# Two layers of attention and FFN on one core: query blocks of 256, value matmuls taken late in a pass through a shared bank, a shorter rsqrt

## Chip, core and metric

One core of a Trainium2 chip. The metric is the device time of one execution in microseconds (us). Ratios are the mean time of one kernel's fast runs over that of the other's fast runs of the same rounds, so not quite the ratio of the medians quoted beside them. A difference under 2%: "same"; intervals are 95%.

Spans come with a mean granted TensorE clock (1.0 is full speed). In profiles PE is TensorE's matmuls, PEld its weight loads, DVE is VectorE, ACT ScalarE and POOL GpSimd.

## The reference

Two layers, each an attention half and an FFN half, on x of 2048 rows by 448, bfloat16, with the same weights in both layers.

```python
x = x + A(layernorm(x))     # 16 heads of 28: softmax(q k^T / sqrt(28)) v, then @ wo
x = x + B(layernorm(x))     # relu(x @ w1 + b1)^2 @ w2 + b2, inner width 1792
```

Each layer has 16 x 2048 x 2048 scores to exponentiate: over two layers 134 million, in tiles of 128 rows 1.05 million columns, which is 683 instructions of 128x1536 (the last of 128x1024).

## The kernel before

A planner inside the kernel places every instruction in order of estimated time. The streams have priorities: scores 0, exponentials 1, value matmuls 2, and the rest ("chains" of projection, layernorm and FFN of a block) from 3 on; junk matmuls, which only keep TensorE's clock up, come last. Four heads make a group g; a "pass" is one block of queries and one g over a range of keys. W1 and W2 stand for the two products of the FFN, rsqrt for the reciprocal square root in the layernorm, and a bank is a unit of PSUM, the memory that the matmuls here write to; the pools below hold eight. The code is abridged:

```python
blocks = [[(0, 4), (4, 4), (8, 4), (12, 4)],            # first tile, tiles of 128 queries
          [(0, 4), (4, 4), (8, 2), (10, 2), (12, 1), (13, 1), (14, 1), (15, 1)]]
ps_sc = tile_pool(bufs=2, PSUM)   # scores, 3 banks each
ps_o  = tile_pool(bufs=1, PSUM)   # one bank for value matmuls
ps_m  = tile_pool(bufs=1, PSUM)   # one bank for QKV, projection, FFN, junk
...
def engs_now(early=False):        # who empties a bank of QKV / W1
    return ("ACT", "DVE") if (early and ("s", 0) not in pl.tok) or len(s_left) == 0 else ("DVE",)
...
def rsqrt(e):                     # 12 instructions on 128 x (1 to 4)
    nc.vector.tensor_scalar(out=v, in0=mv[:, 0:nt, 1], scalar1=EPS, op0=ALU.add)
    nc.vector.tensor_scalar(out=yi, in0=v.bitcast(DT.int32), scalar1=1, op0=ALU.arith_shift_right)
    nc.vector.tensor_scalar(out=yi, in0=yi, scalar1=-1.0, scalar2=float(MAGIC), op0=ALU.mult, op1=ALU.add)
    for _ in range(3):
        nc.vector.scalar_tensor_tensor(out=t, in0=y, scalar=-0.5, in1=y, op0=ALU.mult, op1=ALU.mult)
        nc.vector.tensor_tensor(out=t, in0=t, in1=v, op=ALU.mult)
        nc.vector.scalar_tensor_tensor(out=y, in0=t, scalar=1.5, in1=y, op0=ALU.add, op1=ALU.mult)
...
def e_stream():                   # one exponential over three score banks
    nc.scalar.activation(out=pt[:, 0:n], in_=gbuf[gi]["sc"][:, 0:n], func=AF.Exp, scale=scale)
...
def p_stream():                   # value matmuls of a step as soon as its exponential is done
    o = Op("PE", 0.23 + 0.01 * r, fn, deps=[("e", gis[-1]), ...], acq=R_o if opens else None, ...)
...
def heat():                       # junk matmuls where the planned load falls short
    for gi in range(1, len(groups)):
        short = 0.74 - pl.load(WINDOW)          # WINDOW = 2.8 us
        if short <= 0 or not s_left: continue
        k = 1 if short < 0.14 else 2            # matmuls of 448 columns
```

The softmax here doesn't subtract the row's maximum and nothing guards it: scores larger than these inputs give would overflow.

## Time and profile before

| | median us | spread | profiled span us | clock |
|---|---|---|---|---|
| before | 965.8 | 965.59 to 966.02 | 962.6 | 0.993 |

The prediction below reads the page of this profile: the exponentials on ScalarE run without a break for most of the span. I cut the span at the seventh exponential (27.73 us), after which they run on, and at the end E of the last one (938.98 us). Busy time by these three stages, kernel before; the columns are the stretch, its length, then busy us and instructions of PE, PEld, DVE, ACT and POOL, the TensorE clock, the DMA share and GB/s:

```profile
0.00:27.73 27.73, 23.30 (x131) 10.28 (x134) 20.23 (x71) 14.28 (x14) 7.53 (x16) 1.00 0.82 241
27.73:938.98 911.25, 812.99 (x7962) 304.42 (x8011) 402.58 (x915) 909.60 (x678) 0.00 (x0) 1.00 0.04 11
938.98:962.60 23.62, 17.96 (x174) 12.96 (x173) 10.62 (x32) 5.31 (x11) 0.00 (x0) 0.84 0.05 16
```

The clock column reads 1.00 in the head only because the trace's clock records begin at about 6.2 us: from 1.2 to 6.0 us the first matmuls come every 0.37 us, afterwards every 0.19.

The middle stage is full: 909.60 of 911.25 us on ScalarE. Only the 27.73 and the 23.62 us at the ends and the 1.65 us of gaps can be saved by anything that leaves the exponentials as they are.

### The profile page before, as it was taken

The numbers are of one execution on the slowest core, as the hardware profiler recorded it, in microseconds if no ns is written. First come the engines' busy times: TensorE is split into PE (matmuls) and PEld (weight loads), VectorE is DVE, ScalarE is ACT, GpSimd is POOL, SyncE is SP. The second block draws the span as 40 slices with busy tenths as digits, with TensorE's granted clock in tenths as the row PEclk, the third lists the DMA queues.
The fourth block names the chain that finished last, engine by engine and source line by source line (L and its number), as shares of the span: only waits on it lengthen the run. The fifth ranks groups of instructions, "written<-read, shape, count | busy, mean of one in ns | idle before, by whom it ended". The sixth has DMA issues, their size and how long they took to land.

```text
span 962.6 us, 19338 instructions
## 1 busy us (share of the span) xinstructions
PE 854.3 (89%) x8267; PEld 327.7 (34%) x8318; DVE 433.4 (45%) x1016; ACT 929.2 (97%) x701; POOL 7.5 (1%) x16
## 2 busy tenths in 40 slices
PE   8888899899888998888888999898899889988987
PEld 3333223233232332322323233223233333555555
DVE  7843335434354344653445433325525433444454
ACT  5999999999999999999999999999999999999992
POOL 3000000000000000000000000000000000000000
PEclk9999999999999999999999999999999999999998
DMA  9000010000000000000000000010000000000000
GB/s 276 2 1 1 2 41 7 12 12 13 13 12 1 12 13 13 1 1 1 1 1 1 1 1 1 12 36 24 12 22 17 13 18 22 17 21 13 22 10 16
DMA packets 24642, 17.25 MB, mean 18 GB/s; under 512 B 11754, under 2 KB 21547, under 8 KB 24556
## 3 DMA queue, kind: packets, MB, share of 16 engines
q1 hardware_dynamic: 24556, 16.02, 5.6%
q8 instruction: 65, 1.06, 0.5%
q14 instruction: 21, 0.17, 0.1%
HBM read 13.73 MB, written 2.06 MB: 16 GB/s over the span
## 4 chain that ended last, share of the span: by engine, by line
ACT 68%; issue 18%; PE 12%; DVE 1%; ACTq 0%
ACT pt L558 68%; PE mt L417 4%; PE sc L543 3%; PE oT L593 2%; PE sc L417 1%; PE oT L233 1%; PE mt L763 1%; DVE r L719 1%; PE tp L359 0%; DVE xnT L369 0%; DVE rec L641 0%; DVE x_sb L690 0%; PE den L635 0%; ACT r L717 0%; ACT Q_sb L431 0%
## 5 line engine op out<-in xcount | busy, mean ns | idle before, releaser
L558 ACT ACTIVATE pt<-sc 128x1536 bf16<-128x1536 f32 (+1 forms) x683 | 917.8, 1729 | 6.6 <-PE sc L543 6.5
L543 PE MATMUL sc<-Q_sb,K_sb 32*128 32x512 bf16 (+2 forms) x3072 | 269.2, 309 | 53.8 <-ACT pt L558 45.1
L593 PE MATMUL oT<-pt,V_sb 128*32 128x512 bf16 (+2 forms) x3072 | 206.1, 316 | 1.0 <-ACT pt L558 0.6
L543 PEld LDWEIGHTS <-K_sb 32*128 32x128 bf16 x3072 | 98.3, 91 | 298.9 <-issue 287.3
L417 PE MATMUL mt<-xnT,w 128*128 128x512 bf16 (+2 forms) x565 | 116.6, 321 | 16.7 <-DVE r L719 10.7
L719 DVE TENSOR_SCALAR r<-mt 128x512 bf16<-128x512 f32 x106 | 72.8, 686 | 127.2 <-PE mt L417 127.1
L417 PE MATMUL mt<-w,h 128*128 128x448 bf16 x434 | 102.9, 355 | 2.5 <-DVE x_sb L690 1.0
L593 PEld LDWEIGHTS <-V_sb 128*32 128x32 bf16 x3072 | 62.6, 94 | 110.2 <-issue 103.9
L690 DVE TENSOR_TENSOR x_sb<-x_sb,mt 128x448 bf16<-128x448 bf16 x62 | 38.5, 620 | 136.5 <-PE mt L417 136.0
L763 PE MATMUL mt<-xn,ident 128*128 128x448 bf16 x204 | 68.0, 356 | 9.9 <-DVE xnT L369 1.5
L417 PEld LDWEIGHTS <-w 128*128 128x128 bf16 x672 | 51.3, 101 | 57.0 <-issue 42.1
L417 PEld LDWEIGHTS <-h 128*128 128x128 bf16 x448 | 35.2, 97 | 45.4 <-issue 23.9
L726 DVE TENSOR_TENSOR h<-r 128x512 bf16<-128x512 bf16 x114 | 47.5, 418 | 5.6 <-ACT r L717 2.5
L417 PE MATMUL mt<-xnT,wq 128*128 128x512 bf16 x115 | 34.5, 380 | 7.2 <-DVE Q_sb L433 4.1
L310 DVE BATCH_NORM_STATS2 st<-x_sb 128x6 f32<-128x448 bf16 x64 | 39.7, 621 | 2.2 <-DMA x_sb<-in_A_x_dram 0.8
L433 DVE CAST Q_sb<-mt 128x512 bf16<-128x512 f32 x30 | 20.7, 689 | 37.5 <-PE mt L417 37.4
L433 DVE CAST K_sb<-mt 128x512 bf16<-128x512 f32 x29 | 20.0, 691 | 36.1 <-PE mt L417 36.1
L459 DVE CAST V_sb<-mt 128x448 bf16<-128x448 f32 x31 | 19.3, 621 | 33.7 <-PE mt L417 33.7
L417 PE MATMUL mt<-xnT,wk 128*128 128x512 bf16 x103 | 30.2, 381 | 3.4 <-DVE K_sb L433 0.9
L369 DVE COPY xnT<-tp 128x1024 bf16<-128x1024 bf16 (+1 forms) x31 | 20.8, 672 | 27.2 <-PE tp L359 27.2
L417 PE MATMUL mt<-wo,oTn 128*128 128x448 bf16 x124 | 30.0, 354 | 2.5 <-DVE x_sb L690 1.2
L417 PE MATMUL mt<-wv,xnT 128*128 128x448 bf16 x124 | 29.9, 360 | 2.6 <-DVE V_sb L459 2.0
(75 smaller groups left out, 330.7 us busy)
## 6 DMA issues: line engine op xcount, KB each, us to landing
rec<-scr SPq DMA_DIRECT2D x20, 256.0 KB
x_sb<-in_A_x_dram SPq DMA_DIRECT2D x8, 224.0 KB
out_dram<-x_sb SPq DMA_DIRECT2D x16, 112.0 KB
w<-in_B_w_dram SPq DMA_DIRECT2D x1, 1568.0 KB
w<-in_B_w_dram SPq DMA_DIRECT2D x1, 1344.0 KB
rec<-scr SPq DMA_DIRECT2D x8, 128.0 KB
rec<-scr SPq DMA_DIRECT2D x12, 64.0 KB
part_sb<-in_A_wqkv_dram SPq DMA_DIRECT2D x1, 672.0 KB
```

Of the source, the lines that this page charges most:

```text
L310: nc.vector.bn_stats(out=st[:, :], in_=x_sb[:, t0 + j, :])
L369: nc.vector.tensor_copy(out=dst, in_=tp[:, :, 0:w])
L417: nc.tensor.matmul(box["t"][:, c0:c0 + n], lhsT=lhsT, rhs=rhs, start=a, stop=b)
L433: nc.vector.tensor_copy(out=dst, in_=src)
L459: nc.vector.tensor_copy(out=o, in_=i)
L543: nc.tensor.matmul(sc[:, c0:c0 + nt * P], lhsT=K_sb[l][rows, g, (kb + i) * P:(kb + i + 1) * P], rhs=Q_sb[rows, g, t0 * P:(t0 + nt) * P], s ...
L558: nc.scalar.activation(out=pt[:, 0:n], in_=gbuf[gi]["sc"][:, 0:n], func=AF.Exp, scale=scale)
L593: nc.tensor.matmul(box["t"][DHP * hh:DHP * hh + DHP, 0:n], lhsT=V_sb[l][:, kb + i, 4 * g + hh, :], rhs=gbuf[gi]["pt"][:, c0:c0 + n], start ...
L690: nc.vector.tensor_tensor(out=x_sb[:, tb, :], in0=x_sb[:, tb, :], in1=t[:, 0:D], op=ALU.add)
L719: nc.vector.tensor_scalar(out=r[:, 0:w], in0=t[:, 0:w], scalar1=0.0, scalar2=None, op0=ALU.max)
L726: nc.vector.tensor_tensor(out=h[:, 0:w], in0=r[:, 0:w], in1=r[:, 0:w], op=ALU.mult)
L763: nc.tensor.matmul(t[:, 0:D], lhsT=ident[:, :], rhs=xns[0][:, 0:D], start=True, stop=True)
```

## The change

Its intent, as I read it: shorter blocks give finer work to place, a bank bound to value matmuls becomes a second bank for everything, and VectorE's layernorm gets shorter. It also brings code for a polynomial exponential on VectorE, which is switched off (LAST = 0 lets no group take it). It also changes constants of the planner (SLACK from 0.6 to 0.4, GATE, AHEAD) and several buffer counts. The diff, cut to its core and in places shortened:

```diff
+QR = 256
-MAGIC = 0x5F3759DF
+MAGIC = 0x5F1FFFF9
+LAST = 0            # no exponential on VectorE
+NPT = 11            # buffers of exponentials (before: 4)
+AEND = 8            # ScalarE helps to empty banks until score group 8
+HOLD = 3            # value matmuls wait for 3/8 of a pass ...
+CHUNK = 2           # ... and come two steps at a time
-    blocks = [[(0, 4), (4, 4), (8, 4), (12, 4)], [(0, 4), (4, 4), (8, 2), (10, 2), (12, 1), ... (15, 1)]]
+    blocks = [[(0, 2), (2, 2), ... (14, 2)], [(0, 2), (2, 2), ... (10, 2), (12, 1), (13, 1), (14, 1), (15, 1)]]
-    ps_o = ctx.enter_context(tc.tile_pool(name="ps_o", bufs=1, space=bass.MemoryType.PSUM))
-    ps_m = ctx.enter_context(tc.tile_pool(name="ps_m", bufs=1, space=bass.MemoryType.PSUM))
+    ps_m = [ctx.enter_context(tc.tile_pool(name=f"ps_m{i}", bufs=1, ...)) for i in range(2)]
     def engs_now(early=False):
-        return ("ACT", "DVE") if (early and ("s", 0) not in pl.tok) or len(s_left) == 0 else ("DVE",)
+        return ("ACT", "DVE") if (early and ("s", AEND) not in pl.tok) or len(s_left) == 0 else ("DVE",)
     # rsqrt: 12 instructions become 8
-            nc.vector.tensor_scalar(out=v, in0=mv[:, 0:nt, 1], scalar1=EPS, ...)
-            nc.vector.tensor_scalar(out=yi, ..., op0=ALU.arith_shift_right)
-            nc.vector.tensor_scalar(out=yi, in0=yi, scalar1=-1.0, scalar2=float(MAGIC), ...)
-            for _ in range(3):
+            nc.vector.tensor_scalar(out=v, ..., scalar1=EPS, scalar2=-0.5, op0=ALU.add, op1=ALU.mult)
+            nc.vector.tensor_scalar(out=y.bitcast(DT.int32), in0=v.bitcast(DT.int32), scalar1=-0.5,
+                                    scalar2=float(MAGIC - 2 ** 22 - 2 ** 30), op0=ALU.mult, op1=ALU.add)
+            for k, c in ((1.407904506, 1.6819139), (None, 1.5)):      # three instructions each
...
     def first_block(blk):
-        ... layernorm(4 * blk, 4, ...)
+        ... layernorm(2 * blk, 2, ...)
     # exponentials: log2(e) * 2**23 is folded into Q when its bank is emptied
-                nc.scalar.activation(..., func=AF.Exp, scale=scale)
+                nc.scalar.activation(..., func=AF.Exp, scale=float(np.log(2.0)) * 2.0 ** -23)
     # values
+            hold = 0 if end else max(gi for gi, _, _ in todo[min(HOLD * len(todo) // 8, len(todo) - 1)][1])
+            yield Op("-", 0.0, None, deps=[("e", hold)])
+            while todo:
+                now = [t for t in todo if there(t[1])][:some]         # some = CHUNK
...
-                   acq=R_o if opens else None,
+                       acq=None if "o" in box else pools_now(),
```

## The prediction

> **What bounds the kernel now.** I read the page's busy shares first, then ScalarE alone in order of time, then the chain that ended last, then TensorE around the places where ScalarE stood still.
>
> ```profile
> PE 854.3 (89%) x8267; PEld 327.7 (34%) x8318; DVE 433.4 (45%) x1016; ACT 929.2 (97%) x701; POOL 7.5 (1%) x16
> ACT 68%; issue 18%; PE 12%; DVE 1%; ACTq 0%
> L558 ACT ACTIVATE pt<-sc 128x1536 bf16<-128x1536 f32 (+1 forms) x683 | 917.8, 1729 | 6.6 <-PE sc L543 6.5
> ```
>
> ScalarE is busy 97%, and 917.8 of its 929.2 us is one line: 683 exponentials over three score banks at once. They overlap (683 x 1729 ns is more than 917.8 us), so the pitch, not the mean, is what one costs. The third line also says that in the whole run the exponentials waited only 6.6 us. ScalarE in order of time shows where:
>
> ```profile
> 15.07 6.82 ACT L558 ACTIVATE pt<-sc 128x1536 bf16<-128x1536 f32 x5 [0.49 <-PE sc L543]
> 26.39 463.80 ACT L558 ACTIVATE pt<-sc 128x1536 bf16<-128x1536 f32 x345 [4.49 <-PE sc L543]
> 490.97 428.80 ACT L558 ACTIVATE pt<-sc 128x1536 bf16<-128x1536 f32 x319 [0.78 <-PE sc L543]
> 920.50 18.48 ACT L558 ACTIVATE pt<-sc 128x1536 bf16<-128x1536 f32 x14 [0.73 <-PE sc L543]
> ```
>
> The pitch is 463.80/345 = 1.3443 us. So the span of 962.6 us has three parts: a head until the stream runs without a break (26.39 us, with five exponentials done in it), the stream (678 exponentials, to 938.98), and a tail of 962.6 - 938.98 = 23.6 us with no exponential. The time of 965.8 us is 3.2 us over the span.
>
> The two breaks of 0.7 us deserve a look, TensorE at the first:
>
> ```profile
> 486.54 0.40 PE L593 MATMUL oT<-pt,V_sb 128*32 128x512 bf16 x4
> 487.56 0.61 PE L543 MATMUL sc<-Q_sb,K_sb 32*128 32x512 bf16 x3 [0.62 <-ACT pt L558]
> 488.65 1.67 PE L417 MATMUL mt<-wv,xnT 128*128 128x448 bf16 x4
> 491.04 0.92 PE L417 MATMUL mt<-wv,xnT 128*128 128x448 bf16 x4 [0.17 <-DVE V_sb L459]
> ```
>
> The same four matmuls take 1.67 us and two microseconds later 0.92: TensorE ran at half pace after a stretch in which it did only 0.39 + 0.40 us of work per 1.34 us. The second break (920 us) has the same picture. The junk matmuls of line 763 (204, 68.0 us) are there to prevent this.
>
> [...]
>
> **The change, part by part.**
>
> *Exponentials.* The diff adds a polynomial exponential on VectorE, but its guard asks for a group at or beyond 60 and at most 0, so no group takes it. The order of instructions confirms it: ScalarE still has 682 exponentials of 1536 columns and one of 1024. Folding log2(e) into Q moves a factor. Gain in the stream: 0. That leaves a floor of 682 x 1.344 + 0.95 = 917.7 us, and puts the only possible gains into the 21 us of head, 1.5 us of breaks and 23.6 us of tail.
>
> *Blocks of 256.* Score and value matmuls go from 1536 of 512 columns + 512 of 256 + 1024 of 128 each (3072) to 3584 of 256 + 1024 of 128 (4608): more instructions, same columns. The kernel before already runs this size at 690 to 910 us: six score matmuls of 256 columns take 0.39 us, as three of 512 do, and ScalarE is 100% busy there. So no cost by itself.
>
> *Head.* Only two tiles are normalised first and the rsqrt has 8 instructions, not 12, at about 0.2 us each. I follow it with the durations of before. Statistics of three tiles 3.50 to 5.8; rsqrt 0.2 + 0.35 + 6 x 0.195 = 1.7, to 7.5; the fourth tile's statistics 0.8; two norms 0.7, to 8.95. In the old trace the fourth step would be the transposes at once, but the 34 warm-up matmuls hold TensorE until 10.1 in both kernels, and VectorE's queue has the second block's rsqrt (1.7) ahead of the copy. Copy 10.65 to 11.35, against 12.03 before. From there to the first exponential it was 3.0 us; so 14.4 against 15.07. Then ScalarE does five more copies among the exponentials (K, two V, Q; 0.6 each), and scores queue behind QKV matmuls; by the same durations the sixth exponential starts at about 24.2 and the seventh at 27.3, after which I see no more waits for K or Q. Before, the sixth started at 26.39, so the seventh at 27.73. Gain 0.4 us; the early start is mostly eaten.
>
> *Stream.* From 27.3: 676 x 1.3443 + 0.95 = 909.7, end at 937.0 without breaks. The value matmuls are now withheld until 3/8 of a pass and issued two steps at a time (16 matmuls, 2 x 0.33 us), and the filler goes from 204 to 345. I summed TensorE's work between neighbouring score groups in both orders, with pitches from the trace (0.33 us a value step, 0.19 for 448 columns, 0.11 for 256, 0.36 for a score group): the mean is 1.18 us before and 1.20 after, of 1.344, but carrying over what does not fit, the backlog exceeds 0.5 us at 24 groups before and 83 after, and 0.9 us [...] at 0 and 3. Bunching makes it lumpier. The second shared bank lets FFN matmuls go on while VectorE empties the first, which spares waits of 11 us in all (behind line 719) that did not delay ScalarE. I put the breaks at 2 us, against 1.5. End of stream 939.0.
>
> *Tail.* Before, from the end of the stream E: four rounds of denominators through one bank, the projection of the last block added at E + 6.2, 12 rsqrt instructions with two squares of the block before among them (norm done at E + 11), and W1 only at E + 14.1 because TensorE had W2 of block 14 first. After, block 14's W1 is nearly all done inside the stream. From E: 8 left-over W1 matmuls 0.6, one filler 0.35, two value steps 0.85 (before 0.4 for one), copy 0.3, denominator and reciprocal 1.5, multiply 0.3, meanwhile W2 of block 14 (3.0), projection 0.9, addition done at E + 7.1: later by 0.9. Statistics 0.85, rsqrt 8 x 0.19 = 1.55, norm 0.4, transposes 0.45, copy 0.6: W1 at E + 11.05, earlier by 3.05. Then W1 3.1, W2 3.0, addition 0.6, store 2.7: 20.7. But TensorE now idles from E + 6.5 to E + 10 before W1, while before W2 of block 14 kept it warm. [...] Tail 22.3, against 23.6.
>
> Sum: 939.0 + 22.3 = 961.3 span, + 3.2 = 964.5 us. Against before that is -0.4 in the head, +0.5 in breaks and -1.3 in the tail: -1.2 (with rounding -1.3).
>
> **The rivals.** (a) *TensorE lags in the stream.* For it: backlog at 83 groups, and each spell at half pace cost 0.75 us before. Against: more filler, spare mean, two banks. Five to fifteen such breaks would make 968 to 976; being over 985 would take some 27. (b) *Better overlap in head and tail.* If the tail stays warm and the head has no gap at all, 2 + 3 us more: 959. Nothing lies below: floor 917.7 + at least 12 of head and 16 of tail + 3.2 is 949. (c) *Two banks pay in the stream.* It looks like the intent, but a wait of TensorE that ScalarE did not feel pays nothing; then 964 as said.
>
> **Range and chances.** Head uncertain by 1 us, tail by 2, breaks by -1.5 to +8, skewed upward: 959 to 972. Two per cent is 19.3 us, below 946.5 (under the floor of b) or above 985.1. Faster 0.02, same 0.94, slower 0.04.
>
> **What would show it.** ScalarE in order of time: 683 exponentials with a pitch of 1.344; first at about 14.4; a gap before the seventh that puts it near 27.3; few breaks, each of under 1 us, with TensorE at half pace or behind a bunch of value matmuls; the last one near 939; 22 us after it, with W1 matmuls at 0.11 us each. I am wrong if the pitch differs, if breaks sum to over 5 us, or if the tail is under 20 us.

With the half-pace term of the tail the forecast came to 964.5 us: a tail of 20.7 + 1.6 = 22.3 us, and 939.0 + 22.3 + 3.2; without the term it would have been 962.9. The 1.6 us for the cold clock was my estimate. The half pace itself is in the trace (in the tail 16 W1 matmuls took 1.91 us at 944.31 and 1.06 at 954.87), but how long it would last was not shown: in the same trace it lasted from 1.2 to 6.0 us in the head and, by the clock records, 6.83 us in the tail. The 0.95 us for the last exponential, of 1024 columns, was an estimate too; the 14 exponentials from 920.50 took 18.48 us, which leaves 1.00 after 13 x 1.3443.

## The result, and the profile after

| | median us | runs | ratio to before | profiled span us | clock |
|---|---|---|---|---|---|
| before | 965.91 | 965.59 to 968.5 (4) | | 962.6 | 0.993 |
| after | 961.1 | 959.23 to 962.3 (4) | 0.9943 (0.9918 to 0.9967) | 957.4 | 0.996 |

All outputs are right. A gain of 0.6% is real: the interval lies below 1. The predicted 964.5 us was 3.4 us too high, inside its range.

The page of the changed kernel: busy shares, the chain that ended last, and the group of the exponentials.

```profile
PE 838.9 (88%) x12123; PEld 431.9 (45%) x12123; DVE 443.1 (46%) x1151; ACT 928.7 (97%) x700; POOL 7.6 (1%) x16
ACT 76%; issue 16%; PE 6%; DVE 1%; DMA 0%; ACTq 0%
L633 ACT ACTIVATE pt<-sc 128x1536 bf16<-128x1536 f32 (+1 forms) x683 | 917.8, 1831 | 1.7 <-PE sc L614 1.6
```

Nearly 4000 matmuls more, and ScalarE as before: 683 exponentials, 917.8 us busy. The mean of one grew from 1729 to 1831 ns while their sum stayed; the mean contains overlap (683 x 1831 ns would be 1251 us) and says nothing of the cost. ScalarE in order of time, changed kernel (start, length, instruction, count, and in brackets the idle time before it and what ended it):

```profile
14.35 1.45 ACT L633 ACTIVATE pt<-sc 128x1536 bf16<-128x1536 f32 x1 [0.49 <-PE sc L614]
16.76 5.48 ACT L633 ACTIVATE pt<-sc 128x1536 bf16<-128x1536 f32 x4 [0.49 <-PE sc L614]
23.14 1.46 ACT L633 ACTIVATE pt<-sc 128x1536 bf16<-128x1536 f32 x1
25.84 398.04 ACT L633 ACTIVATE pt<-sc 128x1536 bf16<-128x1536 f32 x296
424.46 511.49 ACT L633 ACTIVATE pt<-sc 128x1536 bf16<-128x1536 f32 x381 [0.59 <-PE sc L614]
```

The pitch is 398.04/296 = 1.345 us, as before. The seventh exponential starts at 25.84, the stream has a single break of 0.59 us, and it ends at E = 424.46 + 511.49 = 935.95. So, against the kernel before:

| part | before | after | difference | predicted |
|---|---|---|---|---|
| head, to the seventh exponential | 27.73 | 25.84 | -1.89 | -0.4 |
| stream | 911.25 | 910.11 | -1.14 | +0.5 |
| of it, breaks | 1.51 | 0.59 | -0.92 | +0.5 |
| tail, from E | 23.62 | 21.45 | -2.17 | -1.3 |

TensorE in the tail, the kernel before. It has the FFN's second matmuls (128x448) of the block before last at 950.24, and then the first ones (W1, 128x128, 56 in all) of the last block, each 0.056 us apart:

```profile
950.24 2.81 PE L417 MATMUL mt<-w,h 128*128 128x448 bf16 x14
953.08 1.95 PE L417 MATMUL sc<-xnT,w 128*128 128x128 bf16 x32
954.87 1.06 PE L417 MATMUL mt<-xnT,w 128*128 128x128 bf16 x16
```

And the changed kernel:

```profile
938.08 2.81 PE L467 MATMUL sc<-w,h 128*128 128x448 bf16 x14
940.92 0.92 PE L467 MATMUL sc<-wo,oTn 128*128 128x448 bf16 x4
945.41 0.40 PE L409 MATMUL tp<-ident,xn 128*128 128x128 bf16 x4 [3.57 <-DVE xn L434]
946.48 1.87 PE L467 MATMUL mt<-xnT,w 128*128 128x128 bf16 x16 [0.67 <-ACT xnT L417]
948.14 2.66 PE L467 MATMUL sc<-xnT,w 128*128 128x128 bf16 x32
```

The same work in another order: the second matmuls of the block before last lie ahead of the last projection (940.92), and W1 starts at E + 10.5, not E + 14.1. But TensorE stands still for 3.57 us while VectorE does the layernorm, and then 16 matmuls take 1.87 us, where 16 took 1.06 before. W1 lasts 4.60 us (946.48 to 951.08) against 3.13 (953.08 to 956.21). The kernel before paid for a cold clock too, but earlier in its tail: 16 matmuls of block 14's W1 took 1.91 us at 944.31.

### The profile page after: what moved, and what is told of

It is laid out like the page before. It is cut to its first block, busy times and chain, and to the rows that moved or that the text cites. A ratio compares the mean times of both kernels' runs of the same rounds, so it can differ in the third digit from the quotient of the medians.

```text
span 957.4 us, 27259 instructions
## 1 busy us (share of the span) xinstructions
PE 838.9 (88%) x12123; PEld 431.9 (45%) x12123; DVE 443.1 (46%) x1151; ACT 928.7 (97%) x700; POOL 7.6 (1%) x16
## 4 chain that ended last, share of the span: by engine, by line
ACT 76%; issue 16%; PE 6%; DVE 1%; DMA 0%; ACTq 0%
ACT pt L633 76%; PE mt L467 2%; PE sc L614 1%; PE sc L467 1%; PE mt L909 1%; PE oT L736 1%; DVE st L357 0%; DMA x_sb<-in_A_x_dram 0%; PE tp L409 0%; DVE xn L434 0%; DVE x_sb L833 0%; ACT Q_sb L482 0%; DVE tt L385 0%; DVE rstd L390 0%; DVE ve L380 0%
## 5 line engine op out<-in xcount | busy, mean ns | idle before, releaser
L633 ACT ACTIVATE pt<-sc 128x1536 bf16<-128x1536 f32 (+1 forms) x683 | 917.8, 1831 | 1.7 <-PE sc L614 1.6
L614 PE MATMUL sc<-Q_sb,K_sb 32*128 32x256 bf16 (+1 forms) x4608 | 270.5, 259 | 93.4 <-ACT pt L633 88.9
L736 PE MATMUL oT<-pt,V_sb 128*32 128x256 bf16 (+1 forms) x4608 | 153.8, 263 | 0.3 <-DVE K_sb L761 0.3
L467 PE MATMUL mt<-xnT,w 128*128 128x256 bf16 (+1 forms) x952 | 123.5, 266 | 6.4 <-DVE r L864 2.2
L864 DVE TENSOR_SCALAR r<-mt 128x512 bf16<-128x512 f32 (+1 forms) x109 | 74.4, 683 | 87.1 <-PE mt L467 86.6
L736 PEld LDWEIGHTS <-V_sb 128*32 128x32 bf16 x4608 | 93.0, 96 | 45.6 <-issue 41.3
L909 PE MATMUL mt<-xn,ident 128*128 128x448 bf16 x345 | 104.2, 358 | 2.4 <-DVE x_sb L833 0.7
L467 PEld LDWEIGHTS <-w 128*128 128x128 bf16 x1008 | 81.4, 99 | 43.9 <-issue 32.7
L833 DVE TENSOR_TENSOR x_sb<-x_sb,mt 128x448 bf16<-128x448 bf16 x62 | 38.2, 616 | 101.2 <-PE mt L467 101.0
L467 PEld LDWEIGHTS <-h 128*128 128x128 bf16 x448 | 34.9, 97 | 43.8 <-issue 22.3
L761 DVE COPY oT_sb<-oT 128x256 f32<-128x256 f32 (+1 forms) x52 | 19.7, 380 | 65.4 <-PE oT L736 64.9
L467 PE MATMUL mt<-xnT,wk 128*128 128x256 bf16 x256 | 36.1, 276 | 2.4 <-DVE xnT L419 2.2
L822 DVE TENSOR_TENSOR oTn<-oT_sb,rec 128x256 bf16<-128x256 f32 (+1 forms) x72 | 27.7, 386 | 20.5 <-DMA rec<-scr 20.3
L467 PE MATMUL mt<-xnT,wq 128*128 128x256 bf16 x240 | 33.8, 274 | 0.6 <-DVE K_sb L488 0.5
L488 DVE CAST K_sb<-mt 128x512 bf16<-128x512 f32 x30 | 20.7, 690 | 28.3 <-PE mt L467 28.1
L484 DVE TENSOR_SCALAR Q_sb<-mt 128x512 bf16<-128x512 f32 x30 | 20.7, 690 | 24.6 <-PE mt L467 23.4
```

Source lines behind the costliest of these rows:

```text
L467: nc.tensor.matmul(box["t"][:, c0:c0 + n], lhsT=lhsT() if callable(lhsT) else lhsT, rhs=rhs, start=a, stop=b)
L484: nc.vector.tensor_scalar(out=dst, in0=src, scalar1=by, scalar2=None, op0=ALU.mult)
L488: nc.vector.tensor_copy(out=dst, in_=src)
L614: nc.tensor.matmul(sc[:, c0:c0 + nt * P], lhsT=K_sb[l][rows, g, (kb + i) * P:(kb + i + 1) * P], rhs=Q_sb[rows, g, t0 * P:(t0 + nt) * P], s ...
L736: nc.tensor.matmul(box["t"][DHP * hh:DHP * hh + DHP, 0:n], lhsT=V_sb[l][:, kb + i, 4 * g + hh, :], rhs=p[:, c0:c0 + n], start=begin and kb ...
L822: nc.vector.tensor_tensor(out=oTn_of[l, qb][0][:, g, 0:n], in0=res["t"][:, 0:n], in1=box["r"][:, 0:n], op=ALU.mult)
```

## The experiments

My theory after the result: the change pays at the two ends only. In the head, it is ScalarE's help (AEND) and the shorter rsqrt; in the tail, the order of work and the rsqrt, less what the cold clock takes back. The stream is at its floor, and its breaks depend on the clock. Rivals: the shorter rsqrt relieves VectorE throughout; the late values or the two banks pay in the stream; the exponentials would be better shared with VectorE.

One experiment could not be made: with one shared bank in the changed kernel the kernel's planner finds no order ("no stream can go on"), so it was never run. The part of the second bank stays open.

All in one table; "7th" is the start of the seventh exponential, the breaks are the gaps after it, the tail is counted from E:

| kernel | 7th | breaks: number, us | tail | span, clock | median us | ratio (95%) |
|---|---|---|---|---|---|---|
| control (the changed kernel) | 25.83 | 6, 3.59 | 21.46 | 961.7, 0.987 | 961.32 | 0.9946 (0.9923 to 0.9969) |
| long_rsqrt | 28.39 | 7, 3.44 | 23.31 | 966.1, 0.987 | 966.95 | 0.9999 (0.9977 to 1.0021) |
| aend0 | 27.36 | 4, 1.36 | 22.42 | 960.9, 0.993 | 962.55 | 0.9957 (0.9936 to 0.9978) |
| values_at_once | 26.99 | 0, 0 | 23.62 | 959.8, 0.996 | 961.54 | 0.9957 (0.9931 to 0.9984) |
| no_filler | 26.32 | 31, 15.48 | 21.79 | 978.8, 0.874 | 984.33 | 1.0194 (1.0162 to 1.0226) |
| vector_exps | 26.39 | 40, 24.05 | 24.39 | 969.0, 0.981 | 970.91 | 1.0045 (1.0020 to 1.0070) |
| tail_warm | 25.84 | 1, 0.52 | 20.01 | 956.0, 0.998 | 958.96 | 0.9924 (0.9901 to 0.9947) |
| last_block_first | 25.96 | 7, 2.98 | 21.88 | 961.0, 0.989 | 961.17 | 0.9934 (0.9901 to 0.9966) |
| tail_both | 26.12 | 3, 1.32 | 19.02 | 956.7, 0.995 | 959.32 | 0.9936 (0.9920 to 0.9952) |
| tail_both_filler | 26.44 | 2, 0.50 | 18.46 | 954.8, 0.998 | 956.68 | 0.9907 (0.9892 to 0.9922) |
| before_short_rsqrt | 27.46 | 4, 3.88 | 22.03 | 963.5, 0.991 | 963.15 | 0.9966 (0.9943 to 0.9988) |
| before_256 | 28.11 | 9, 5.32 | 20.07 | 964.1, 0.988 | 963.98 | 0.9979 (0.9964 to 0.9994) |

In the rounds the kernel before had a median of 966.45 us (control, long_rsqrt, values_at_once, tail_warm), 966.44 (no_filler, vector_exps, last_block_first, before_short_rsqrt; these eight on one chip), 965.59 (tail_both, tail_both_filler, before_256; on a second chip) and 966.78 (aend0; on a third). The ratio is the number to compare.

### control: the changed kernel once more

No edit.

> The changed kernel unaltered, as the yardstick of this chip. All theories: 959 to 962 us against 965.5 to 968.5 of the kernel before. Its trace should repeat head and tail to 0.2 us (first exponential near 14.35, seventh near 25.8; 21.4 us after the last one); only the breaks in the stream may differ from run to run[...].

The head and tail are those of the first profile to 0.01 us. The breaks are not: 3.59 us instead of 0.59, in the same program. One of them, ScalarE first, then TensorE, control:

```profile
141.80 1.45 ACT L633 ACTIVATE pt<-sc 128x1536 bf16<-128x1536 f32 x1 [0.34 <-PE sc L614]
144.16 1.45 ACT L633 ACTIVATE pt<-sc 128x1536 bf16<-128x1536 f32 x1 [0.91 <-PE sc L614]
```

```profile
143.45 0.61 PE L614 MATMUL sc<-Q_sb,K_sb 32*128 32x256 bf16 x6
143.99 1.49 PE L467 MATMUL mt<-xnT,w 128*128 128x256 bf16 x8
145.42 0.39 PE L614 MATMUL sc<-Q_sb,K_sb 32*128 32x256 bf16 x6
```

Six score matmuls take 0.61 us and a little later 0.39. Busy time by stretch from 140 to 148 us (columns as in the table of stages), control and then the first profile of the changed kernel:

```profile
140.00:148.00 8.00, 7.54 (x96) 4.32 (x95) 2.48 (x5) 6.44 (x6) 0.00 (x0) 0.69 0.06 19
```

```profile
140.00:148.00 8.00, 6.70 (x122) 3.89 (x120) 3.80 (x8) 8.00 (x8) 0.00 (x0) 1.00 0.07 19
```

A clock of 0.69 here and 1.00 there, 96 matmuls here and 122 there: the break goes with a stretch in which the granted clock was lower. In which executions that happens is not a matter of the program alone, which is the same in both. Over the ten listed executions of the changed kernel the span falls from 961.7 us at clock 0.987 to 957.4 at 0.996, with a correlation of -0.98. So most of the spread between runs goes with the clock.

The traces' clock records say where they come from. They list spells at clock 0.5, each 3.41 us long or a multiple of it: one in the stream of the first profile (420.55 to 423.96), four (20.5 us in all) in control's. In the first profiles of both kernels every change of the clock inside the span comes a multiple of 3.413 us after the one before: 2.80 us past such a multiple in the kernel before, 0.71 in the changed one, counted from the start of the span. Of the 46 breaks in the streams of all traces but those of no_filler and vector_exps, 43 lie in a spell or end within 1.5 us of one. I cut each of the 14 traces from 30 to 935 us into consecutive stretches of 3.413 us, in step with its spells. In the 54 stretches at full clock that a spell followed, TensorE was busy 33 to 67% by the trace (52 of them under 65%); of the 3532 that none followed, none was under 59%, and 33 were under 65%. This was worked out after the runs, and no experiment set the load on purpose. My reading, which these numbers fit but no run proves: the program fixes where TensorE's load dips under about 60%, and the phase of the stretches (2.80 and 0.71 us above) decides which dip costs a spell.

Kernels whose load dips alike are best compared at equal clock: at 0.991 fifteen listed executions of the kernel before, on three chips, span 962.9 to 964.9 us (on control's chip 964.3 to 964.7) and two of the changed kernel 959.9, so 3 to 5 us less; the two ends differ by 1.89 + 2.17 = 4.06. (The mean clock contains the cold stretch of the tail, 3.8 us' worth before and 2.1 after, so this comparison is good to about a microsecond. An edit that changes TensorE's load can change the clock itself, as no_filler does below (0.874), and a comparison at equal clock leaves that effect out.)

### long_rsqrt: the old rsqrt in the changed kernel

The edit in words:

```diff
-            8 instructions, two refining steps
+            12 instructions, three refining steps, as in the kernel before
```

> Only the rsqrt is undone: 12 instructions on VectorE again instead of 8. Theory A (ScalarE's pitch fixes the stream, the gain is made at the two ends): two rsqrts lie ahead of the first block's copy in the head (+1.5 us) and one on the path of the tail (+0.8 us), nothing in the stream though 34 rsqrts get longer; so +1.5 to +2.5 us over the control, about 963. Theory B (the short rsqrt is the whole gain, by relieving VectorE everywhere): +5 us, back at 966. Theory C (the gain is TensorE's better flow by the second bank and the bunched values): about 0.

The median gives back all of the gain: 966.95 us. Its place is the two ends: head +2.56 us, tail +1.85, together 4.4, as is the difference of spans at the same clock (966.1 and 961.7 at 0.987). The stream without its breaks is 910.96 us against 910.8 of control: nothing, although VectorE was busy 18.6 us longer. In the head, VectorE's copy that TensorE waits for; changed kernel, then long_rsqrt:

```profile
10.58 0.68 DVE L419 COPY xnT<-tp 128x1024 bf16<-128x1024 bf16 x1
```

```profile
12.16 0.68 DVE L418 COPY xnT<-tp 128x1024 bf16<-128x1024 bf16 x1
```

1.58 us later, because two rsqrts (the first and second block's) lie ahead of it in VectorE's order, each four instructions of 0.195 us longer. The first exponential moves by the same 1.58 (15.93), and by the seventh the shift has grown to 2.56. In the tail, one rsqrt on the chain moves the transposes from E + 9.46 to E + 10.48; the other 0.9 us is the end of the last store, which took 3.6 us here and 2.6 to 2.8 in the other 13 traces, so I do not put it down to the edit. That leaves 2.56 + 1.02 = 3.6 us for the edit in this trace; why the head moves by 2.56 and not by 1.58, and the rest of the median's 5.6 us, stay open. So the theory of the ends has the place right and expected too little (1.5 to 2.5); the rival of relief everywhere named a total near the measured median, but its mechanism is not there.

### aend0: ScalarE stops helping when the scores start

```diff
-AEND = 8
+AEND = 0
```

> The changed kernel with ScalarE's help in the head ended at the first score group (AEND 0, as in the kernel before) instead of the ninth: the K, V and Q copies that ScalarE squeezed between the first exponentials go to VectorE, which is busy with statistics and rsqrts there. If those copies on ScalarE are what makes the head shorter, the seventh exponential comes 1 to 3 us later than 25.8 us (27 to 29), and the time is 962.5 to 964.5. If they only cost ScalarE time (2.4 us of copies), it comes earlier, about 24.5.

As expected. The first exponential is where it was (14.35), the seventh 1.5 us later:

```profile
27.36 310.63 ACT L633 ACTIVATE pt<-sc 128x1536 bf16<-128x1536 f32 x231 [2.43 <-PE sc L614]
```

So 1.5 of the head's 1.89 us hang on ScalarE's copies among the exponentials (K, two V, Q), which it makes where it would have waited. The two parts do not add up: with ScalarE's help but the old rsqrt (28.39) the head is longer than that of the kernel before.

### values_at_once: value matmuls as soon as they can

```diff
-HOLD = 3
-CHUNK = 2
+HOLD = 0
+CHUNK = 1
```

> Values are taken as their exponentials come, one step at a time (HOLD 0, CHUNK 1), still in one of two shared banks. Theory A: the stream is at ScalarE's pitch either way, so the time stays within 1 us of the control. Theory C (withholding and bunching gives the gain): +3 to +5 us, most of the way back to the kernel before. My own backlog estimate in the prediction would have bunching cost about 1 us: then -1.

```profile
26.99 909.19 ACT L633 ACTIVATE pt<-sc 128x1536 bf16<-128x1536 f32 x677 [0.19 <-PE sc L614]
```

Not one break in 909.19 us, with 203 junk matmuls instead of 345, and no spell at half clock in the stream. The late, bunched values do not pay in the stream; by the traces they cost there, as the prediction feared, though through the clock. Let a stretch of 3.413 us start anywhere in the stream: TensorE's load falls under 60% for 1.9 us of starting times in this trace, and for 9.4 and 9.2 us in the two traces of the changed kernel. Divided by 3.413 that makes an estimated 0.6 spells in a run against 2.7. But the planner's order shifts at the ends: head +1.15, tail +2.17. Of the latter, 1.0 is W1 starting later (E + 11.53), and 1.07 is W1 at half pace for longer (5.67 us instead of 4.60). At equal clock (0.996) this kernel spans 959.2 to 959.8 us against 957.4, and 963.7 against 961.7 at 0.987: about 2 us slower. The median is only 0.2 us higher, because its executions have higher clocks (five of six at 0.993 or more, against three of ten), which the estimate above makes the edit's own gain rather than luck. What HOLD and CHUNK buy is thus a different order at the ends.

### no_filler: no junk matmuls in the stream

```diff
-    pl.spawn(9.5, heat())
```

> All 345 junk matmuls (104 us of TensorE's busy time) are gone. Theory A with the clock behind the breaks: the breaks in the stream, 0.6 to 3.6 us in the runs so far, grow to 5 to 20 us, each with TensorE at half pace, and the mean granted clock falls below 0.95; time 966 to 980. Rival: the breaks come from bunched value matmuls and backlog, and fillers only add to it; then the time falls by 1 to 3 us.

The largest effect of all, +23 us, and more than I expected (the verdict against before is "unclear", as the interval contains 2%). The stream of this kernel, busy time by stretch:

```profile
26.00:957.00 931.00, 792.12 (x11502) 399.03 (x11497) 414.44 (x1052) 914.86 (x679) 0.00 (x0) 0.87 0.05 12
```

TensorE does less (792.12 us against 802.23 in the same stretch of the changed kernel), at a clock of 0.87, and ScalarE waits: 31 breaks of 15.48 us in sum, and the rest of the 21 us in waits too short to be listed.

### vector_exps: a third of some groups on VectorE

```diff
-LAST = 0
+LAST = 660
```

> The guard is opened (LAST 660): in 57 groups VectorE takes the third of the three banks with the polynomial, ScalarE does 1024 columns instead of 1536. If ScalarE's pitch is what sets the stream, 57 x 512 columns / 1.2 per ns = 24 us come off: 937 us. If TensorE or VectorE is as close to its limit (VectorE goes from 443 to about 680 us busy), the gain is under 10 us: above 951.

(The 1.2 columns per ns agree with the trace: the shortest exponential, of 1024 columns, took 1.017 us, one of 1536 by itself 1.45, so 512 columns 0.43.)

Neither expectation gave the right sign. 57 groups had their third bank taken by the polynomial. ScalarE's busy time in the exponentials fell by 16.6 us, from 917.8 to 901.2, and the time rose by 9.6. The group of the exponentials, and ScalarE at the longest gap, vector_exps:

```profile
L633 ACT ACTIVATE pt<-sc 128x1536 bf16<-128x1536 f32 (+1 forms) x683 | 901.2, 1508 | 26.4 <-DVE vi L645 13.1
```

```profile
416.66 9.08 ACT L633 ACTIVATE pt<-sc 128x1024 bf16<-128x1024 f32 x7 [3.65 <-DVE vi L645]
```

Before it, VectorE and TensorE in the same trace:

```profile
414.84 0.54 PE L909 MATMUL mt<-xn,ident 128*128 128x448 bf16 x2 [3.21 <-DVE x_sb L833]
415.31 0.40 PE L614 MATMUL sc<-Q_sb,K_sb 32*128 32x256 bf16 x6
415.89 0.68 DVE L645 TENSOR_SCALAR vi<-sc 128x512 int32<-128x512 f32 x1
```

ScalarE was idle for 26.4 us before exponentials instead of 1.7. In this trace the two readers of a group's scores never overlap: in 50 of the 57 groups the exponential starts 0.03 to 0.09 us after VectorE has read its third (vi), in the other 7 vi comes after the exponential. So where VectorE is behind with other work, ScalarE waits for it; 13.1 of the 26.4 us ended with vi. Another 12.0 us ended with score matmuls, and the stream has eight spells at half clock. The longest gap has both kinds: junk matmuls waited 3.21 us for VectorE's addition to x (L833), the score matmuls came after them (415.31), and only then vi, until 416.57. VectorE was busy 66% only: with a third of its time free it was still late for its turn. Whether the two readers must take turns, or this program makes them, no run shows; so what is shown is that this way of sharing does not pay.

### tail_warm: TensorE kept busy during the last layernorm

```diff
+        if l == 1 and qb == len(blocks[1]) - 1:      # after the last projection
+            (in words:) 16 junk matmuls of 448 columns, into a free bank
```

> 16 junk matmuls of 448 columns between the last projection and the last transposes, where TensorE idled 3.6 us. If W1 of the last block was slow because the clock had dropped (48 matmuls at about 0.095 us in 946.5 to 950.8 instead of 0.056), W1 now takes 3.1 instead of 4.8 us and the tail is 1.6 us shorter: about 959.5, tail 19.8 us. If W1 was slow for weight loads or waits for a bank, nothing is gained (0), or 0.2 is lost.

```profile
941.71 3.19 PE L854 MATMUL mt<-xn,ident 128*128 128x448 bf16 x16
945.45 0.40 PE L409 MATMUL tp<-ident,xn 128*128 128x128 bf16 x4 [0.55 <-DVE xn L434]
946.51 1.95 PE L467 MATMUL sc<-xnT,w 128*128 128x128 bf16 x32 [0.67 <-ACT xnT L417]
```

W1 starts where it did (E + 10.5) and its first 32 matmuls take 1.95 us, the full pace (1.95 at 953.08 in the kernel before). The tail is 20.01, 1.44 us less than the changed kernel's, which is the half-pace term by itself.

### last_block_first: the last block's chain ahead of block 14's

```diff
-            pl.spawn(4 + 0.1 * qb, chain(l, qb))
+            pl.spawn(3.6 if l == 1 and qb == len(blocks[1]) - 1 else 4 + 0.1 * qb, chain(l, qb))
```

> The last block's chain goes ahead of the one before it: the last projection is issued after 8 of the 14 W2 matmuls of block 14, not after all and the bias. If this projection is on the path that ends last, the tail is 1.2 to 1.4 us shorter (about 20.1 us instead of 21.4), and some of W1's slow clock stays. If the path is set by W2 of block 14 or by stores, nothing.

```profile
947.63 0.61 PE L409 MATMUL tp<-ident,xn 128*128 128x128 bf16 x4 [2.63 <-DVE xn L434]
950.57 3.62 PE L467 MATMUL sc<-xnT,w 128*128 128x128 bf16 x32
```

The transposes come at E + 8.5, 0.95 us earlier. But 32 matmuls now take 3.62 us instead of 2.66, the half pace to the last; W1 lasts 5.7 us, and the tail is 21.88: in this execution the gain went into the slower W1. Not in every one: two others span 956.4 and 956.7 us at clock 0.996, where the changed kernel has 957.4.

### tail_both and tail_both_filler: the order and the warmth

tail_both is the two edits together, with 13 junk matmuls. tail_both_filler adds:

```diff
-            short = 0.74 - pl.load(WINDOW)
+            short = 0.84 - pl.load(WINDOW)
```

> The last block's projection goes ahead and 13 junk matmuls fill the gap before the transposes. With last_block_first alone the transposes came 0.95 us earlier after the last exponential (8.51 against 9.46 us) but W1 took 5.7 us instead of 4.6. If the clock took that gain back, the tail is now 19.0 us (W1 3.1 us), 2.4 us under the control: about 958.5. If the two gains do not add, 20.0 us as with the junk alone.

> As tail_both, with the target of TensorE's load for the junk matmuls of the stream raised from 0.74 to 0.84 (482 instead of 345 of them). If the breaks are the clock's, they fall to under 0.5 us in every run, the runs spread less than 1.5 us, and the median is 1 to 3 us under tail_both: 956 to 957.5. If more junk crowds the scores, breaks appear at full clock and the time rises.

The tail of tail_both is 19.02 us: together the edits give 2.4 us, where singly they gave 1.4 and -0.4 (one profile of each). Its median, 959.32, has the breaks of an ordinary run. With more junk matmuls (482 for 345) the breaks nearly go, and TensorE's load falls under 60% for 2.8 us of starting times instead of tail_both's 9.4. ScalarE, tail_both_filler:

```profile
26.44 115.63 ACT L633 ACTIVATE pt<-sc 128x1536 bf16<-128x1536 f32 x86
142.29 1.45 ACT L633 ACTIVATE pt<-sc 128x1536 bf16<-128x1536 f32 x1 [0.22 <-PE sc L614]
144.02 792.32 ACT L633 ACTIVATE pt<-sc 128x1536 bf16<-128x1536 f32 x590 [0.28 <-PE sc L614]
```

Its four executions have clocks of 0.995 to 1.0 and times of 956.49 to 957.85 us. Of its gain, 0.56 us is again an order of the tail (18.46 us; the last projection starts at E + 2.75, not E + 3.65). It is the fastest kernel here, 0.9907 (0.9892 to 0.9922) of the kernel before, where the changed kernel had 0.9946 (0.9923 to 0.9969) in control's rounds, on another chip.

### before_short_rsqrt and before_256: parts of the change in the kernel before

The first puts the eight-instruction rsqrt into the kernel before. The second splits three of the four blocks of the first layer there:

```diff
-    blocks = [[(0, 4), (4, 4), (8, 4), (12, 4)], ...
+    blocks = [[(0, 4), (4, 2), (6, 2), (8, 2), (10, 2), (12, 2), (14, 2)], ...
```

> The kernel before with the short rsqrt alone, blocks of 512 and all else as it was. If the short rsqrt is worth by itself what its undoing cost in the changed kernel (4.4 to 5.6 us): 961. My reading: in the old head the warm-up matmuls hold the transposes until 10.1 us anyway, and in the old tail W1 of the last block waits for W2 of the one before, so little of it is felt: -0.3 to -1.5 us, 964.5 to 966.

> The kernel before with blocks of 256 queries in the first layer except its first block, all else as it was. If blocks of 256 cost or gain nothing in the stream, as I took it, within 1.5 us of the kernel before (head and tail the same: 26.4 and 23.6 us). If they are part of the gain (chains shorter, K and V of the second layer earlier), -2 to -4; if 1.5 times as many score and value matmuls load TensorE, breaks and +2 to +5.

The short rsqrt alone measured 963.15 us, better than I expected. By its profile the head gains 0.27 us and the tail 1.6. At equal clock the gain is 0.8 to 2.2: spans of 962.5 and 963.5 us at 0.991 where the kernel before, on the same chip, has 964.3 to 964.7. TensorE's load falls under 60% about as often in both (6.5 and 7.0 us of starting times), so part of the 3.3 us of the median is luck with the clock. In the head of the kernel before, only one rsqrt lies ahead of VectorE's first copy, and that copy then waits 0.34 us for TensorE's transposes behind the warm-up matmuls; so little of a shorter rsqrt is felt there. The tail's 1.6 us goes with another order of the last matmuls.

before_256 gained 1.6 us, all of it in a tail of 20.07 us that the planner ordered otherwise, against a later head (+0.4) and 5.3 us of breaks. It does not isolate the block size, since that cannot be changed without moving everything behind it. What the size is worth by itself stays open.

## Why the prediction was right

**The bound and the floor held.** The pitch is unchanged, no exponential was moved, ScalarE's 917.8 us are the same to the tenth, and no part of the change lowered the stream's floor. That made "same" safe.

**Head: right mechanism, size missed by 1.5 us.** The copy came at 10.58 (predicted 10.65) behind the second rsqrt, as said, and the first exponential at 14.35 (14.4). That it fits to 0.07 us is partly luck: the first rsqrt took 2.17 us (5.61 to 7.78), not 1.7, and the statistics, norms and second rsqrt (1.46) less than assumed. The sixth came at 23.14, not 24.2, and the seventh at 25.84, not 27.3. The mis-sized term is "by the same durations": I charged each QKV tile its whole shown duration, about 1.05 us (this sum is not written out in the prediction). TensorE in the head, changed kernel:

```profile
21.00 0.92 PE L467 MATMUL mt<-wv,xnT 128*128 128x448 bf16 x4
21.76 0.92 PE L467 MATMUL sc<-wv,xnT 128*128 128x448 bf16 x4
22.61 0.39 PE L614 MATMUL sc<-Q_sb,K_sb 32*128 32x256 bf16 x6
```

Each is listed with 0.92 us, but the next starts 0.76 and 0.85 us after it. Six tiles between the second and the sixth exponential took 5.1 us from start to start, not 6.3, which covers the 1.06 us by which the sixth came early; the seventh gained another 0.4. "The early start is mostly eaten" was therefore wrong; it was kept. (The prediction's "21 us of head" that could be gained is 19.7, 27.73 - 6 x 1.344; the 21 contain the 1.5 us of breaks that it lists beside them.)

**Stream: the predicted 2 us of breaks was about an ordinary run, and the profile was a lucky one.** It shows 0.59, control shows 3.59. If the ends stay as they are, a span s of the changed kernel has about s - 956.8 us of breaks; over the ten listed spans the median is 2.7, an estimate. (It includes waits too short to be listed: for control it gives 4.9, where 3.59 are listed.) For the kernel before the same estimate (s - 961.1) gives 1 to 8 us, median 3.5. So "+0.5" has the wrong sign, if any, and rival (a), a lagging TensorE with 5 to 15 breaks, did not come: at full clock the backlog at 83 groups that I summed delayed next to nothing (3 of 46 breaks lie outside the spells). What bunching costs, by my reading it costs through dips in load (9.4 and 9.2 us of starting times under 60%, 1.9 in values_at_once, which had no spell). What goes with a break was named rightly, TensorE at half pace (43 of 46 breaks lie in a spell or end within 1.5 us of one); that it is drawn anew in each run of the same program I had not seen. Nor that the 3.2 us I added from span to time were 1.8 us of constant and 1.4 us by which the profiled run (964.36 us) lay below the median.

**Tail: right, with a sum mended.** The half-pace term was predicted as 1.6 us and measured as 4.60 - 3.13 = 1.47, and tail_warm takes it away by itself (1.44). From the end of W1 to the end, 6.3 was predicted and 6.32 measured. The sums are off, however: the terms from the addition to W1 make E + 10.95, not 11.05, and those after it make 20.45, not the 20.7 written, so 22.05 with the cold clock's 1.6. And W1 started at E + 10.53 rather than E + 11.05, since the addition to x was done at E + 6.56, not 7.1 (value matmuls 0.63 us, not 0.85, and less waiting between). Against the kernel before W1 starts 3.57 us earlier; undoing the rsqrt takes back 1.02 of it, and the rest is the planner's order, which no run isolates.

**Sum.** Against 964.5: head -1.46, stream 910.11 for 911.7, so -1.6, tail -0.85, and 3.7 us from the profiled span to the median for 3.2, so +0.5: -3.4, to 961.1.

**Rivals (b) and (c).** (b), better overlap at the ends, named 959 for "2 + 3 us more" if the tail stays warm and the head has no gap, without saying which is which. Of the head's, 1.5 came; the tail's came only once it was kept warm (20.01 us in tail_warm, 19.02 in tail_both, for the predicted 22.3). (c), that the two banks pay nothing in the stream, is compatible with all runs but not shown: the one-bank kernel could not be built.

## What to carry to other kernels

Where one engine is full for 95% of the span, add up the ends and look there: a small instruction on the one chain before the first and after the last of its work counts in full or more (four instructions of 0.2 us, twice in the head and once in the tail, moved the seventh exponential by 2.6 us and the last transposes by 1.0), while nearly all of the same 18.6 us of VectorE time lay in between and counted nothing. Check that it is on the chain: in the head of the kernel before the same edit moved 0.27 us. Moving work earlier on TensorE can leave it idle and then slow (here 3.57 us idle, then 16 matmuls in 1.87 us instead of 1.06); fill the hole with junk matmuls before counting the gain, for in the profiles here each edit alone gave less than both (1.4 and -0.4 us against 2.4). When differences are smaller than what changes with the clock from run to run of one program (here 957.4 us at 0.996 and 961.7 at 0.987), compare kernels over many runs, or at equal clock if the edit leaves TensorE's load as it was.
